# Step 3's decayed r and k are transposed by transfers, and the engine orders from word 50 on are new

## The chip, the cores and the metric

The kernel runs on one core of one Trainium2 chip. The metric is the device time of one execution in microseconds: 182.38 as the median of three runs of the kernel before (181.91 to 182.72). Five engines work side by side, each through its own queue in order: TensorE (PE, with its weight loads as PEld), VectorE (DVE), ScalarE (ACT), GpSimd (POOL) and SyncE (SP), which here issues all DMA transfers.

## What is computed

A linear attention with a decay per channel and a state (RWKV-6), and behind it a dense layer with squared relu:

```python
for t in range(S):                                   # B, H, S, D = 4, 8, 768, 48
    cur = einsum('bhd,bhe->bhde', u[None] * kt, vt)
    y[:, :, t] = einsum('bhd,bhde->bhe', rt, state + cur)
    state = wt[:, :, :, None] * state + einsum('bhd,bhe->bhde', kt, vt)
x = y as [3072, 384]
out = relu(x @ w_in) ** 2 @ w_out                    # w_in [384, 2048], w_out [2048, 384]
```

Inputs and output are float32; the matmuls run in bf16.

## The kernel before

The 3072 tokens are cut into 12 steps (0 to 11) of 256 tokens, three steps for each of the four sequences; a step has two chunks of 128, and each partition row holds two neighbouring tokens. For a step the attention goes this way: products of w (`ww_`), their logarithm (`lw_`), sums of it along the chunk by matmuls with triangles (`cum_`), the exponential (`exp_`, `ac_`), decayed r and k (`rd_.s.0` and `rd_.s.1`, lines 351 to 364), r and k transposed, their products for all pairs of tokens (`p_.s.0` and `p_.s.1`, line 420) times a mask (`pm_`), the states (`su_`, `ts_`, `sn_`), and y from the masked products and v (`y_`) and from r and the states (`yc_`), summed with a diagonal part (`q_`, `vq_`) in `ysb_`. For the dense layer y is transposed (`yt_` and its copy `xt_`, or one transfer, `dyt_`), multiplied with w_in in eight words of six matmuls (`m1_.s.0` to `m1_.s.7`, line 536), taken through relu (`rl_`) and square (`sq_.s.q`, each over two of the eight), multiplied with w_out in eight words of four matmuls (`m2_.s.c.q` for chunk c and quarter q, line 564), scaled (`os_`) and stored.

Decayed r and k can be transposed in two ways. `tr_` does it with eight matmuls against the identity into a PSUM bank (line 376), and `rkt_` copies the bank to SBUF (lines 391 and 393). `dtr_` issues one DMA that reads SBUF and writes SBUF:

```python
def dtr_(s, i):
    t = new_rkt(s, i)
    if i == 0:
        nc.sync.dma_start_transpose(out=t[:],
                                    in_=tiles["rdec", s][0][:].rearrange("t a j e d -> t (a j e d)"))
    else:
        nc.sync.dma_start_transpose(out=t[:].rearrange("p j a t -> p (j a) t"),
                                    in_=tiles["rdec", s][1][:].rearrange("t j h d -> t (j h d)"))
```

Before, steps 0 to 3 use `tr_` and `rkt_`, and steps 4 to 11 use `dtr_`.

Nothing is scheduled by a program at build time. The string ORDER lists words, and the loop at line 598 runs them one after the other; each appends its instructions to the queues of its engines. So the words' order is, engine by engine, the order of the instructions. A word reads `name.step.parts:bank=engine`: `rkt_.3.1=V` copies the transposed k (1; r is 0) of step 3 on VectorE (A is ScalarE, G is GpSimd). Banks `0` to `3` are single PSUM banks; `cum_`, `p_`, `su_` and `y_` use pairs of banks, `att0` and `att1` (`0` and `1` there), or the single banks in pairs (`b` is 0 and 1, `m` is 2 and 3). `warm_.n.i` are n matmuls on nothing that keep TensorE busy at the start. `ld.s.x` loads w, r, k or v of a step, or a part of w_in (`ld.n.i`) or w_out (`ld.n.o`), each of four; `cast.i.n` and `cast.o.n` make them bf16.

```python
for word in ORDER.split():
    word, _, engine = word.partition("=")
    word, _, banks = word.partition(":")
    name, *args = word.split(".")
    args = tuple(int(x) if x.isdigit() else x for x in args)
```

Of the kernel before, what the change touches and what calls it, by code (L numbers as in the profile page):

```python
# [20 lines left out]
ts_.0.0=A kw_.1=G pm_.0.0 pm_.0.1 vs_.0.0=A sn_.0.0 ld.1.i exp_.1 rw_.1=G vs_.0.1=A qs_.0=A rd_.1.1 ku_.1=G  # L21
warm_.3.2 yc_.0.1:1 ld.0.i ac_.1 ts_.0.1=V rd_.1.0 warm_.2.2 tr_.1.1:0 sn_.0.1 y_.0:1 rkt_.1.1=A vq_.0=V
tr_.1.0:1 ww_.2=G ld.2.i v_.1=A rkt_.1.0=V ysb_.0=V vs_.1.1=A warm_.4.2 p_.1.1:0 qp_.1=G su_.1:m ld.2.v
pm_.1.1 lw_.2 yt_.0:0 cum_.2:1 ld.3.i ts_.1.0=V rw_.2=G q_.1 exp_.2 kw_.2=G xt_.0=V vs_.1.0=A rd_.2.0 qs_.1=G
ac_.2 cast.i.1=A rd_.2.1 warm_.10.1 tr_.2.0:1 sn_.1.0 p_.1.0:0 ku_.2=G ts_.1.1=V yc_.1.1:1 tr_.2.1:0
cast.i.0=A pm_.1.0 ld.0.o m1_.0.3:2 ld.3.w rkt_.2.1=V m1_.0.2:3 vq_.1=G rkt_.2.0=V y_.1:1 rl_.0.3=A yc_.1.0:1
rl_.0.2=V p_.2.0:0 m1_.0.1:2 ld.1.o ysb_.1=V cast.i.2=G m1_.0.0:3 rl_.0.1=A pm_.2.0 yt_.1:0 ld.3.r rl_.0.0=A
m1_.0.5:2 v_.2=A xt_.1=V qp_.2=G sn_.1.1 m1_.0.4:3 rl_.0.5=A p_.2.1:1 su_.2:b sq_.0.0=A rl_.0.4=V ld.2.o
m1_.1.4:2 cast.i.3=G ts_.2.0=V pm_.2.1 m1_.1.5:3 rl_.1.4=A q_.2 sn_.2.0 m1_.1.3:2 rl_.1.5=A ld.3.o vs_.2.1=G
vs_.2.0=A yc_.2.0:0 yc_.2.1:0 rl_.1.3=V m1_.1.6:3 cast.o.0=G qs_.2=A m1_.1.0:2 ld.3.k rl_.1.6=V sq_.0.2=A  # L30
y_.2:0 rl_.1.0=V m1_.1.1:3 vq_.2=G m1_.1.7:2 rl_.1.1=V ld.3.v m2_.0.1.0:0 sq_.1.2=A rl_.1.7=V sq_.0.1=A
cast.o.1=G m1_.1.2:3 rl_.1.2=A ysb_.2=V m1_.0.7:2 ld.4.w ww_.3=G yt_.2:1 rl_.0.7=V m1_.0.6:3 xt_.2=V m2_.0.1.1
sq_.1.1=A rl_.0.6=V ld.5.w m1_.2.6:2 cast.o.2=G lw_.3 sq_.1.0=A rl_.2.6=A cum_.3:1 sq_.1.3=A rw_.3=G al_.3
ld.5.r m2_.0.0.0:1 m1_.2.7:3 m2_.0.0.1 cast.o.3=V exp_.3 sq_.0.3=A ld.4.k rd_.3.0 kw_.3=G m1_.2.1:2 rl_.2.7=A
ac_.3 m2_.0.1.2 m2_.0.0.2 rl_.2.1=V ku_.3=G m2_.0.0.3 rd_.3.1 ld.4.v m2_.0.1.3 vs_.3.0=A m1_.2.0:3 os_.0.1=V
qp_.3=G ld.5.v m1_.2.3:2 os_.0.0=V rl_.2.0=V tr_.3.1:0 rl_.2.3=A tr_.3.0:1 rkt_.3.1=V v_.3=A ld.4.r m1_.2.4:3
ww_.4=G rkt_.3.0=V m2_.1.0.0:0 rl_.2.4=A q_.3 ww_.5=G p_.3.1:0 vs_.3.1=A ld.6.k su_.3:1 pm_.3.1 p_.3.0:m
m2_.1.0.1 ts_.3.0=A lw_.4 sn_.3.0 ld.5.k pm_.3.0 m2_.1.0.2 qs_.3=A m2_.1.1.0:1 sq_.2.0=A vq_.3=G ts_.3.1=V
m2_.1.0.3 ld.6.w cum_.4:0 m2_.1.1.1 ku_.4=G ac_.4 al_.4 store.0.1 m1_.2.5:2 os_.1.0=A v_.5=A yc_.3.1:1 y_.3:1
lw_.5 kw_.4=G m1_.2.2:3 ld.6.r ysb_.3=V rl_.2.5=A m2_.1.1.2 exp_.4 sn_.3.1 rl_.2.2=V yt_.3:0 rw_.4=G cum_.5:1  # L40
xt_.3=V m2_.1.1.3 vs_.4.0=A ac_.5 sq_.2.1=A qp_.4=G al_.5 m1_.3.0:2 rd_.4.1 v_.4=A m1_.3.3:3 rd_.4.0 dtr_.4.1
m2_.2.0.0:0 rl_.3.0=A rw_.5=G rl_.3.3=A m2_.2.0.1 os_.1.1=V exp_.5 q_.4 dtr_.4.0 su_.4:0 sq_.2.2=A m1_.3.4:2
kw_.5=G rd_.5.0 ww_.6=G m2_.2.1.0:1 rl_.3.4=A ts_.4.0=V sq_.2.3=A m1_.3.5:3 vs_.4.1=A rd_.5.1 sn_.4.0
m2_.2.1.1 store.1.0 ts_.4.1=V rl_.3.5=V ku_.5=G m1_.3.6:2 store.1.1 m2_.2.1.2 qs_.4=A ld.7.w ld.6.v rw_.6=G
p_.4.1:1 rl_.3.6=A p_.4.0:0 pm_.4.1 pm_.4.0 m2_.2.1.3 lw_.6 vq_.4=G m1_.3.1:3 m1_.3.2:2 rl_.3.1=A su_.5:1
dtr_.5.1 dtr_.5.0 vs_.5.1=G sq_.3.0=A rl_.3.2=V yc_.4.0:0 yc_.4.1:0 sn_.4.1 y_.4:0 os_.2.1=V sq_.3.1=A
m1_.3.7:3 ysb_.4=V ld.7.v m2_.2.0.2 rl_.3.7=A ld.8.w kw_.6=G vs_.5.0=G yt_.4:1 ld.7.k sq_.3.3=A m2_.2.0.3
xt_.4=V cum_.6:0 al_.6 m1_.4.4:2 qp_.5=G os_.2.0=A ac_.6 m1_.4.7:3 ts_.5.0=V exp_.6 rl_.4.4=V m2_.3.0.0:1
rl_.4.7=A rd_.6.1 m1_.4.6:2 rd_.6.0 m2_.3.0.1 dtr_.6.1 m2_.3.1.0:0 ku_.6=G qp_.6=G sq_.3.2=A rl_.4.6=A q_.5
dtr_.6.0 p_.5.0:1 p_.5.1:0 vs_.6.0=A m1_.4.5:3 sn_.5.0 m2_.3.0.2 qs_.5=G rl_.4.5=A pm_.5.1 pm_.5.0 vq_.5=G  # L50
m1_.4.1:2 m1_.4.3:3 rl_.4.3=A store.2.1 ld.8.v m2_.3.0.3 rl_.4.1=V ld.8.k v_.6=A ww_.7=G y_.5:0 q_.6 os_.3.0=A
ld.7.r m1_.4.0:3 store.0.0 ld.9.k ww_.8=G yc_.5.0:0 qs_.6=A su_.6:1 yc_.5.1:0 ysb_.5=V vs_.6.1=A ts_.6.0=V
m1_.4.2:2 ld.8.r m2_.3.1.1 rl_.4.0=V yt_.5:1 xt_.5=V sn_.6.0 lw_.7 vq_.6=G rl_.4.2=A p_.6.0:0 m2_.3.1.2
sq_.4.3=A store.2.0 pm_.6.0 m1_.5.2:3 ku_.7=G m1_.5.6:2 ts_.6.1=V yc_.6.1:0 sq_.4.0=A rl_.5.2=A p_.6.1:1
rl_.5.6=A m2_.3.1.3 kw_.7=G pm_.6.1 sq_.4.2=A m1_.5.4:3 rw_.7=G m1_.5.3:2 os_.3.1=V rl_.5.4=A y_.6:0 sn_.6.1
rl_.5.3=A cum_.7:1 kw_.8=G ysb_.6=V al_.7 m2_.4.0.0:1 vs_.7.1=A m1_.5.7:3 m1_.5.5:2 v_.7=G dyt_.6 sq_.4.1=A
rl_.5.7=V qp_.7=G rl_.5.5=V m2_.4.1.0:0 exp_.7 ld.9.w ld.9.v m2_.4.0.1 ac_.7 rd_.7.0 sq_.5.1=A m2_.4.0.2
ku_.8=G rd_.7.1 sq_.5.3=A dtr_.7.0 m2_.4.0.3 m1_.5.0:3 lw_.8 m1_.5.1:2 rw_.8=G rl_.5.0=V su_.7:0 q_.7
rl_.5.1=A cum_.8:1 dtr_.7.1 m1_.6.3:3 qs_.7=A m1_.6.5:2 rl_.6.3=V ld.10.w qp_.8=G ac_.8 sq_.5.0=A m2_.4.1.1
os_.4.0=V ts_.7.0=V ld.11.w sn_.7.0 m1_.6.4:3 rl_.6.5=A al_.8 ww_.9=G m2_.4.1.2 ld.9.r rl_.6.4=V exp_.8  # L60
store.3.0 m2_.5.1.0:1 sq_.5.2=A rd_.8.1 ts_.7.1=V sn_.7.1 m1_.6.0:2 vs_.7.0=G vs_.9.1=A rd_.8.0 m2_.4.1.3
m2_.5.1.1 kw_.9=G rl_.6.0=A dtr_.8.0 p_.7.1:0 v_.8=A p_.7.0:1 vq_.7=G pm_.7.1 m1_.6.1:3 m2_.5.1.2 rl_.6.1=A
pm_.7.0 ku_.9=G m2_.5.1.3 sq_.6.0=A lw_.9 m1_.6.6:2 dtr_.8.1 store.3.1 q_.8 yc_.7.0:0 v_.9=A yc_.7.1:0
rl_.6.6=V rw_.9=G su_.8:1 y_.7:0 os_.5.1=A ts_.8.0=V m1_.6.2:3 ysb_.7=V os_.4.1=A cum_.9:1 m1_.6.7:2 al_.9
dyt_.7 m2_.5.0.0:1 rl_.6.2=V exp_.9 ww_.10=G rl_.6.7=V m2_.5.0.1 ac_.9 ld.10.r rd_.9.1 sq_.6.1=A sq_.6.2=A
sn_.8.0 qp_.9=G ld.10.k qs_.8=G store.4.1 m2_.5.0.2 ld.10.v rd_.9.0 m2_.5.0.3 m2_.6.1.0:0 vs_.8.1=G sq_.6.3=A
dtr_.9.0 vs_.8.0=A p_.8.0:m p_.8.1:0 pm_.8.0 su_.9:1 m2_.6.1.1 ts_.9.0=A pm_.8.1 m2_.6.1.2 lw_.10 m1_.7.4:2
rw_.10=G os_.5.0=V m1_.7.0:3 rl_.7.4=V sn_.9.0 vq_.8=G yc_.8.1:0 dtr_.9.1 yc_.8.0:0 rl_.7.0=V y_.8:0 m1_.7.1:2
q_.9 rl_.7.1=A ts_.9.1=V m2_.6.1.3 kw_.10=G ysb_.8=V m1_.7.7:3 sq_.7.0=A ww_.11=G cum_.10:1 dyt_.8 rl_.7.7=V
m1_.7.5:2 qs_.9=A al_.10 m2_.6.0.0:1 v_.10=G rl_.7.5=A m1_.7.2:3 exp_.10 ld.11.k vs_.9.0=G m2_.6.0.1 lw_.11  # L70
rd_.10.0 rd_.10.1 m1_.7.3:2 rl_.7.2=A vq_.9=G ac_.10 m2_.6.0.2 os_.6.1=A rl_.7.3=A vs_.10.0=A store.6.1
m1_.7.6:3 store.5.1 ku_.10=G m2_.6.0.3 vs_.10.1=A ld.11.r sn_.9.1 rl_.7.6=V m1_.8.5:2 dtr_.10.0 p_.9.1:0
rl_.8.5=A p_.9.0:1 qp_.10=G pm_.9.1 m1_.8.3:3 m2_.7.0.0:0 rl_.8.3=A pm_.9.0 m1_.8.4:2 sq_.7.1=A m1_.8.2:3
os_.6.0=A y_.9:0 sq_.7.3=A rl_.8.2=V yc_.9.1:0 rw_.11=G su_.10:1 m2_.7.1.0:1 sq_.7.2=A ts_.10.0=V ysb_.9=V
m2_.7.1.1 rl_.8.4=A ku_.11=G q_.10 m1_.8.7:3 dyt_.9 m1_.8.1:2 rl_.8.7=V cum_.11:0 dtr_.10.1 kw_.11=G sn_.10.0
rl_.8.1=A m2_.7.1.2 al_.11 m1_.8.0:3 exp_.11 ld.11.v qs_.10=G ts_.10.1=V sn_.10.1 vq_.10=G m1_.8.6:2 rl_.8.0=A
store.6.0 rd_.11.0 m2_.7.1.3 rl_.8.6=A rd_.11.1 m1_.9.4:3 sq_.8.0=A ac_.11 dtr_.11.0 m1_.9.1:2 qp_.11=G
rl_.9.4=V sq_.8.2=A m2_.7.0.1 os_.7.1=V p_.10.1:1 sq_.8.1=A p_.10.0:0 pm_.10.1 store.5.0 dtr_.11.1 store.7.1
m1_.9.0:3 v_.11=G pm_.10.0 vs_.11.1=G m2_.8.1.0:1 rl_.9.0=A rl_.9.1=A m2_.8.1.1 sq_.8.3=V m1_.9.5:3 m2_.7.0.2
m2_.7.0.3 os_.7.0=A yc_.10.0:1 yc_.10.1:1 rl_.9.5=V su_.11:0 y_.10:1 m1_.9.2:2 ysb_.10=V m1_.9.6:3 rl_.9.2=A  # L80
ts_.11.0=V dyt_.10 m2_.8.0.0:0 rl_.9.6=V sn_.11.0 m1_.9.3:2 q_.11 m2_.8.1.2 rl_.9.3=A yc_.11.0:1 vs_.11.0=A
p_.11.1:0 yc_.11.1:1 p_.11.0:m m2_.8.0.1 pm_.11.0 m2_.8.0.2 pm_.11.1 sq_.9.1=A m2_.8.0.3 m2_.8.1.3 qs_.11=A
sq_.9.0=A m1_.9.7:2 os_.8.1=A vq_.11=G y_.11:1 sq_.9.2=A rl_.9.7=V m1_.10.0:3 sq_.9.3=V m2_.9.0.0:1 rl_.10.0=A
m1_.10.5:2 os_.8.0=A store.8.0 store.8.1 m2_.9.0.1 m1_.10.4:3 rl_.10.5=A rl_.10.4=A sq_.10.2=V m2_.9.0.2
# [550 lines left out]
```

## Time and profile before

| | us |
|---|---|
| three timed runs, median | 182.38 |
| the profiled execution | 182.57 |
| its span, first to last instruction | 180.8 |
| TensorE busy | 171.2 |
| ScalarE, VectorE, GpSimd busy | 132.4, 129.7, 122.8 |

A page of the profile gives for each engine its busy time, share and instructions; the chain of waits follows back from the last instruction what released what. A group's row names the line, the engine, the operation, out<-in with the shapes, the count, and behind the bar the busy time, the mean length of one in ns, the idle time ahead of them and what ended it. Lines are those of the kernel before; the changed kernel has one line less in ORDER, so its lines are one lower.

### The profile page before, as it was taken

To read this page: it belongs to the slowest core of one execution; us is meant where nothing else is said; L and a number is where in the kernel's file an instruction comes from. 1 tells how busy PE (TensorE), PEld (TensorE's weight loads), DVE (VectorE), ACT (ScalarE), POOL (GpSimd) and SP (SyncE) were. 2 spreads that over 40 slices of the span, in tenths; PEclk is the share of its full clock that TensorE was granted. 3 is DMA by queue.
4 is the path that set the end of the run, shared out by engine and by line. 5 is a ranking of instruction groups with operands and counts; after the bars stand their busy time and mean duration, and the time that the engine had idled before them with its cause. 6 is when DMAs were issued, how large, how long until landed. Compare 5 with 4: busy or idle time off the path is not lost.

```text
span 180.8 us, 5682 instructions
## 1 busy us (share of the span) xinstructions
PE 171.2 (95%) x2382; PEld 123.2 (68%) x2385; DVE 129.7 (72%) x195; ACT 132.4 (73%) x235; POOL 122.8 (68%) x140
## 2 busy tenths in 40 slices
...
GB/s 147 270 261 232 221 369 350 340 332 302 228 271 217 280 228 215 208 218 255 270 137 237 197 287 101 303 141 143 190 106 244 92 47 0 92 151 22 0 87 130
DMA packets 78952, 35.81 MB, mean 198 GB/s; under 512 B 72144, under 2 KB 77392, under 8 KB 78928
## 3 DMA queue, kind: packets, MB, share of 16 engines
...
## 4 chain that ended last, share of the span: by engine, by line
PE 78%; SPq 10%; DMA 5%; ACT 4%; DVE 1%; issue 1%; ACTq 0%
PE bk L564 33%; PE m L536 33%; SPq L180 8%; DMA w_st<-in_moe_w_in_dram 5%; PE att L420 3%; PE att L483 3%; PE att L493 2%; PE att L446 1%; ACT gt L545 1%; PE bk L516 1%; PE att L328 1%; ACT wi_sb L202 1%; SPq L190 1%; SPq L207 1%; ACT gt L553 1%
## 5 line engine op out<-in xcount | busy, mean ns | idle before, releaser
L536 PE MATMUL m<-xT,wi_sb 128*128 128x256 bf16 x576 | 74.0, 273 | 0.8 <-ACT gt L545 0.7
L564 PE MATMUL bk<-wo_sb,gt 128*128 128x384 bf16 x384 | 72.0, 326 | 0.0
L536 PEld LDWEIGHTS <-wi_sb 128*128 128x128 bf16 x576 | 54.8, 98 | 12.5 <-issue 0.9
L564 PEld LDWEIGHTS <-gt 128*128 128x128 bf16 x384 | 36.9, 98 | 19.2
L545 ACT ACTIVATE gt<-m 128x512 f16<-128x512 f32 x56 | 32.9, 594 | 21.6 <-PE m L536 21.1
L553 ACT ACTIVATE gt<-gt 128x1024 bf16<-128x1024 f16 x42 | 43.3, 1051 | 1.4 <-DVE gt L547 1.1
L547 DVE TENSOR_SCALAR gt<-m 128x512 f16<-128x512 f32 x40 | 27.1, 687 | 9.6 <-PE m L536 9.3
L434 DVE TENSOR_TENSOR pmT<-att,mask 128x1024 bf16<-128x1024 f32 x20 | 23.9, 1218 | 3.9 <-PE att L420 3.9
L299 POOL TENSOR_TENSOR ku<-k_raw,u_bc 128x768 f32<-128x768 f32 x12 | 21.8, 1819 | 0.4 <-DMA u_bc<-in_u_dram 0.4
L304 POOL TENSOR_TENSOR ku<-ku,r_raw 128x768 f32<-128x768 f32 x11 | 20.6, 1877 | 0.2
L318 POOL TENSOR_TENSOR ku<-v_sh,qs 128x768 f32<-128x768 bf16 x11 | 16.2, 1477 | 4.9 <-ACT qs L279 4.8
L279 ACT CAST v_sh<-v_raw 64x384 bf16<-64x384 f32 x34 | 17.3, 508 | 0.4
L292 POOL TENSOR_TENSOR k_raw<-k_raw,w_raw 128x384 f32<-128x384 f32 x12 | 12.1, 1010 | 6.3 <-DMA k_raw<-in_k_dram 6.2
L461 POOL TENSOR_TENSOR S<-t_state,ac_buf 128x192 bf16<-128x192 f32 x20 | 10.2, 508 | 8.1 <-DVE t_state L456 5.7
L504 DVE TENSOR_TENSOR y_sb<-att,ku 128x768 bf16<-128x768 f32 x12 | 11.4, 954 | 5.5 <-PE att L483 1.7
L288 POOL TENSOR_TENSOR r_raw<-r_raw,w_raw 128x384 f32<-128x384 f32 x12 | 12.0, 997 | 3.6 <-DMA r_raw<-in_r_dram 3.6
L363 DVE TENSOR_TENSOR kdec_buf<-k_raw,att 128x768 bf16<-128x768 f32 x12 | 11.4, 950 | 3.5 <-ACT att L342 2.9
L360 DVE TENSOR_TENSOR rdec_buf<-r_raw,att 128x384 bf16<-128x384 f32 x24 | 12.2, 548 | 2.2 <-ACT ac_buf L348 1.1
L342 ACT ACTIVATE att<-att 128x768 f32<-128x768 f32 x12 | 9.6, 799 | 3.4 <-PE att L330 2.0
L571 ACT ACTIVATE o_sb<-bk 128x384 f32<-128x384 f32 x13 | 6.2, 484 | 7.3 <-PE bk L564 7.3
L309 DVE TENSOR_REDUCE q<-ku 128x16 f32<-128x768 f32 x12 | 11.3, 944 | 0.0
L581 PE MATMUL att<-warm 128*128 128x512 bf16 x27 | 8.9, 487 | 1.2 <-DVE half_ones L230 1.2
...
## 6 DMA issues: line engine op xcount, KB each, us to landing
...
w_st<-in_moe_w_in_dram SPq DMA_DIRECT2D x4, 768.0 KB, 9.8
w_st<-in_moe_w_out_dram SPq DMA_DIRECT2D x4, 768.0 KB, 9.0
...
```

What stands on the lines that cost most here:

```text
L180: nc.sync.dma_start(out=t[:, hs, at:at + 2, :].rearrange("p h j d -> p h (j d)"), in_=src[b, hs, i * T:(i + 1) * T, :].rearrange("h (p j) ...
L279: copy(out[j * Q:(j + 1) * Q, c], src[c * Q:(c + 1) * Q, :, j])
L299: tensor_mul("ku_", s, h)(tiles["ku", s][:, hs], raw["k", s][:, hs, 1:3, :], u_bc[:, hs, None, :].to_broadcast([C, n, 2, D]))
L304: tensor_mul("qp_", s, h)(ku, ku, raw["r", s][:, heads(h), 0:2, :])
L318: tensor_mul("vq_", s)(vq[:], tiles["vs", s][:], tiles["qs", s][:, :, :, None].to_broadcast([C, 2, H, D]))
L360: nc.vector.tensor_mul(rdec[0][:, ps, j, :, 0:D], x[:, :, j, :].rearrange("p (a e) d -> p a e d", e=2), dec.rearrange("p (a e) d -> p a e ...
L434: nc.vector.tensor_mul(pmT, ps_p[:].rearrange("p e (x t) -> p (e x) t", t=C), mk.to_broadcast([C, 8, C]))
L536: nc.tensor.matmul(ps1[:, j, :], wi_sb[:, n // 4, kk, n % 4 * 128:(n % 4 + 1) * 128], tiles["xT", s][:, :, kk, :], start=(kk == 0), stop=( ...
L545: nc.scalar.activation(rl, m1, AF.Relu, scale=RS)
L547: nc.vector.tensor_scalar(out=rl, in0=m1, scalar1=RS, scalar2=0.0, op0=ALU.mult, op1=ALU.max)
L553: nc.scalar.activation(gt, rl, AF.Square)
L564: nc.tensor.matmul(m2, gt[:, 4 * q + n, c * C:(c + 1) * C], wo_sb[:, 4 * q + n, :], start=(summed[s, c] == 1 and n == 0), stop=(summed[s, ...
```

## The change

All that differs is ORDER. Its first 50 words, up to `qs_.0`, are the same; behind them the words stand in a new order, with new engines and banks. Four words go and two come:

```diff
-tr_.3.1:0 tr_.3.0:1 rkt_.3.1=V rkt_.3.0=V
+dtr_.3.1 dtr_.3.0
```

Of all others there are as many as before. Some have another engine: relus (`rl_`) on ScalarE are 65 and were 56, squares there 37 and were 42; scalings (`os_`) there 17 and were 13; four words of `ku_` and `kw_` that GpSimd had go to VectorE, and three `qp_` too. `m1_` used banks 2 and 3 and `m2_` banks 0 and 1; now both use all four.

In three places the order shows what the prediction speaks of. The first is SP, the queue of all transfers, where step 3 ends and step 4 begins. Before (from v of step 3 on; then w of steps 4 and 5, r of 5, k of 4, and so on up to the first transposing transfer, of step 4):

```order
L180 DMA v_raw<-in_v_dram 128x8x96
L180 DMA w_raw<-in_w_dram 128x8x96 x2
L180 DMA r_raw<-in_r_dram 128x8x96
L180 DMA k_raw<-in_k_dram 128x8x96
L180 DMA v_raw<-in_v_dram 128x8x96 x2
L180 DMA r_raw<-in_r_dram 128x8x96
L180 DMA k_raw<-in_k_dram 128x8x96 x2
L180 DMA w_raw<-in_w_dram 128x8x96
L577 DMA out_dram<-o_sb 128x384
L180 DMA r_raw<-in_r_dram 128x8x96
L403 DMA_TRANSPOSE kT<-kdec_buf_108 128x8x128
```

And after, from v of step 3 too:

```order
L179 DMA v_raw<-in_v_dram 128x8x96
L195 DMA w_st<-in_moe_w_out_dram 128x4x384
L179 DMA r_raw<-in_r_dram 128x8x96
L195 DMA w_st<-in_moe_w_out_dram 128x4x384
L179 DMA w_raw<-in_w_dram 128x8x96
L402 DMA_TRANSPOSE kT<-kdec_buf_110 128x8x128
L399 DMA_TRANSPOSE rT<-rdec_buf_109 128x8x128
L179 DMA w_raw<-in_w_dram 128x8x96
L179 DMA k_raw<-in_k_dram 128x8x96
L179 DMA r_raw<-in_r_dram 128x8x96
```

The two transposing transfers of step 3 stand behind w of step 5 and ahead of w, k and r of step 4; before, all loads of step 4 were in the queue by then.

The second place is VectorE at the start, in step 1 and the first words of step 2 (`pmT` are mask products, `kdec` and `rdec` decayed k and r, `y_sb` is y, `gt` a relu's result). Before, from the first mask product of step 1:

```order
L434 TENSOR_TENSOR pmT_467<-att0_86,mask_100 128x1024
L456 TENSOR_TENSOR t_state_484<-S_369,m1_0_90 128x192
L309 TENSOR_REDUCE q_487<-ku_331 128x16
L521 COPY xT_491<-bk0_88 128x768
L360 TENSOR_TENSOR rdec_buf0_107<-r_raw_222,att1_87 128x4x2x48 x2
L363 TENSOR_TENSOR kdec_buf0_108<-k_raw_299,att1_87 128x16x48
L456 TENSOR_TENSOR t_state_543<-S_523,m1_1_91 128x192
L434 TENSOR_TENSOR pmT_467<-att0_86,mask_100 128x1024
L393 COPY kT_582<-bk0_88 128x1024
L391 COPY rT_592<-bk1_89 128x1024
L547 TENSOR_SCALAR gt_573<-m1_1_91 128x512
L504 TENSOR_TENSOR y_sb_652<-att1_87,ku_590 128x768
```

And after:

```order
L433 TENSOR_TENSOR pmT_441<-att1_87,mask_100 128x1024
L455 TENSOR_TENSOR t_state_482<-S_409,m1_0_90 128x192
L359 TENSOR_TENSOR rdec_buf0_107<-r_raw_222,att0_86 128x4x2x48 x2
L362 TENSOR_TENSOR kdec_buf0_108<-k_raw_299,att0_86 128x16x48
L455 TENSOR_TENSOR t_state_514<-S_489,m1_1_91 128x192
L433 TENSOR_TENSOR pmT_441<-att1_87,mask_100 128x1024
L392 COPY kT_584<-m1_1_91 128x1024
L503 TENSOR_TENSOR y_sb_611<-att0_86,ku_498 128x768
L433 TENSOR_TENSOR pmT_674<-att1_87,mask_100 128x1024
L520 COPY xT_677<-bk0_88 128x768
```

The reduction `q_.1`, the copy of the first y transposed and the copy of r of step 2 have left this stretch, and no relu stands in it any more.

The third place is ScalarE where the relus and squares of step 4 are (`gt_1558` before, `gt_1562` after; relus read a PSUM bank, squares read `gt`; `v_sh` and `v_bf` are casts of v). Before:

```order
L545 ACTIVATE gt_1558<-m1_1_91 128x512
L553 ACTIVATE gt_1251<-gt_1251 128x1024
L545 ACTIVATE gt_1558<-m1_0_90 128x512
L279 CAST v_sh_1644<-v_raw_1380 64x384 x2
L545 ACTIVATE gt_1558<-m1_1_91 128x512 x2
L274 CAST v_bf_1693<-v_raw_1380 128x8x2x48
L571 ACTIVATE o_sb_1715<-bk1_89 128x384
L279 COPY qs_1746<-q_1713 64x8 x4
L279 CAST v_sh_1644<-v_raw_1380 64x384 x2
L270 ACTIVATE lw_buf1_102<-ww_1695 128x8x48
L545 ACTIVATE gt_1558<-m1_0_90 128x512
L553 ACTIVATE gt_1558<-gt_1558 128x1024 x2
```

And after:

```order
L544 ACTIVATE gt_1562<-m1_1_91 128x512
L278 CAST v_sh_1675<-v_raw_1264 64x384 x4
L278 CAST v_sh_1712<-v_raw_1558 64x384 x2
L544 ACTIVATE gt_1562<-m1_0_90 128x512
L544 ACTIVATE gt_1562<-bk0_88 128x512
L273 CAST v_bf_1743<-v_raw_1558 128x8x2x48
L544 ACTIVATE gt_1562<-bk1_89 128x512
L544 ACTIVATE gt_1562<-m1_0_90 128x512
L552 ACTIVATE gt_1562<-gt_1562 128x1024
L453 COPY t_state_1807<-att1_87 128x192
L552 ACTIVATE gt_1562<-gt_1562 128x1024
```

Between the first relu of step 4 and its first square stood five casts of v, and now stand seven; the copies `qs_` and the logarithm that stood there have moved behind or ahead.

The words of TensorE that go with it, in ORDER, are few lines of the diff's new side: first step 3, then the dense layer of step 4.

```diff
+ld.5.w cast.o.2=A rw_.3=G sq_.0.2=V rd_.3.0 vs_.3.1=G sq_.1.2=V ts_.3.0=V ac_.3 ww_.5=V m2_.0.0.2 sn_.3.0
+sq_.2.3=A m2_.1.1.2 os_.0.0=A qp_.3=V ts_.3.1=V q_.3 os_.1.1=A dtr_.3.1 dtr_.3.0 m2_.0.1.2 p_.3.1:1 p_.3.0:0
...
+p_.6.1:0 qp_.6=V rl_.4.5=A sq_.4.3=A m1_.4.0:1 ww_.8=G xt_.5=V ts_.6.0=A sn_.6.0 m2_.4.0.3:2 m1_.5.2:3 ld.7.w
```

140 lines of the change are left out of this document (68 added, 72 removed).

## The prediction, made before the changed kernel ran

> **What bounds the kernel now.** I read the busy shares of the page first, then stretches by window, then the chain of waits, then the engines that feed TensorE. The first two views (a stretch's row has its mean length, then busy time and instructions of PE, PEld, DVE, ACT and POOL, the granted clock, the DMA share and GB/s):
>
> ```profile
> PE 171.2 (95%) x2382; PEld 123.2 (68%) x2385; DVE 129.7 (72%) x195; ACT 132.4 (73%) x235; POOL 122.8 (68%) x140
> ```
> ```profile
> 60.00:84.00 24.00, 24.00 (x409) 17.89 (x405) 20.47 (x31) 20.90 (x40) 22.93 (x27) 1.00 1.12 229
> 84.00:108.00 24.00, 24.00 (x367) 17.74 (x354) 19.89 (x30) 22.33 (x39) 21.37 (x21) 1.00 1.05 229
> 108.00:132.00 24.00, 23.92 (x384) 17.92 (x381) 19.42 (x30) 18.88 (x36) 20.43 (x25) 1.00 0.79 173
> ```
>
> TensorE is busy in all but 0.1 us from 60 to 132, at full granted clock, and no other engine is. "Busy" can hide waiting, because the ends of matmuls are modelled, so I check it by pace, in the chain of waits (start, length, what):
>
> ```profile
> 18.95 9.05 DMA w_st<-in_moe_w_in_dram
> 28.03 1.47 ACT wi_sb L202
> 29.50 0.51 ACT gt L545
> 30.05 1.47 PE m L536 x12
> 31.52 0.33 PE bk L516 x6
> ...
> 38.23 1.31 PE m L536 x12
> ...
> 50.57 0.89 PE bk L376 x16
> ...
> 170.26 7.16 PE bk L564 x44
> 177.50 0.49 ACT o_sb L571
> ```
>
> 44 matmuls of `m2_` in 7.16 us are 0.163 us each, so a word of four is 0.65 us. Twelve of `m1_` in 1.31 us are two words of 0.655. From 30.05 on the work is 94 words of `m1_` (61.6 us), 96 of `m2_` (62.4) and some 20 us of small matmuls of the attention, 144 to 145 us; the clock shows 30.05 to 177.4, 147.3. No more than 3 us of that is waiting or switching: **TensorE alone sets the time from 30 us to the end**. Ahead of 30 it is the second part of w_in: it lands at 28.0 and is cast by 29.5. The tail behind the last matmul (a scaling and a store) is the same in both versions.
>
> The Trainium skill, "Perfetto Trace Analysis", Identifying the Most-Contended Engine, speaks against this reading: matmul busy time is a bad measure, and the share of weight loads a better one. That share is 68% here, by which a third of TensorE would be free and matmuls taken away worth nothing; the sum below would be 0.9 higher, 183.1. The even 0.163 us a matmul decides against it here.
>
> **The change, part by part.** The sums stand against the profiled execution: 182.57 us, of which 180.8 are the span and 1.77 lie around it. The runs shown have the median 182.38, 0.2 less.
>
> *The transposes of step 3 leave TensorE.* Sixteen matmuls go, the row of 0.89 us at 50.57, in the stretch that TensorE sets: **−0.89**. The two copies out of PSUM go too, on VectorE (the second like the first):
>
> ```profile
> L391 DVE COPY rT<-bk 128x1024 bf16<-128x1024 bf16 x3 | 2.0, 680 | 0.0
> ...
> L391 ACT COPY rT<-bk 128x1024 bf16<-128x1024 bf16 x1 | 1.0, 1012 | 0.1
> ```
>
> Those 1.4 us of an engine that has 4 us of slack in each 24 count as 0.
>
> *The two transfers that come for them* stand in SP's one queue, now ahead of the loads of step 4. Rows of before, for issue and for landing:
>
> ```profile
> 33.99 3.42 SPq L196 DMA_DIRECT2D w_st<-in_moe_w_out_dram  x2
> ...
> 40.64 5.38 SPq L180 DMA_DIRECT2D w_raw<-in_w_dram  x2
> ...
> 62.73 1.33 SPq L403 DMA_TRANSPOSE kT<-kdec_buf  x1
> 64.18 1.27 SPq L400 DMA_TRANSPOSE rT<-rdec_buf  x1
> ```
> ```profile
> w_st<-in_moe_w_out_dram SPq DMA_DIRECT2D x4, 768.0 KB, 9.0
> ...
> kT<-kdec_buf SPq DMA_TRANSPOSE x8, 3.9
> rT<-rdec_buf SPq DMA_TRANSPOSE x8, 4.2
> ```
>
> A transpose takes 1.3 us to issue and 4 us from there to landing. Will it be there in time? The last load of w_out had 12 MB with it and ahead of it in before (12 loads of 0.39, u with 0.2, eight parts of weights of 0.79 and two more loads of 0.39); it was issued in the second half of the row at 33.99 and landed near 45. In the new order r of step 3 ends the same 12 MB (seven parts of weights, four loads of step 3): 45. GpSimd then has r·w behind three operations:
>
> ```profile
> L299 POOL TENSOR_TENSOR ku<-k_raw,u_bc 128x768 f32<-128x768 f32 x12 | 21.8, 1819 | 0.4 <-DMA u_bc<-in_u_dram 0.4
> ...
> L288 POOL TENSOR_TENSOR r_raw<-r_raw,w_raw 128x384 f32<-128x384 f32 x12 | 12.0, 997 | 3.6 <-DMA r_raw<-in_r_dram 3.6
> ...
> L279 POOL CAST v_sh<-v_raw 64x384 bf16<-64x384 f32 x14 | 7.5, 537 | 0.6
> ...
> L274 POOL CAST v_bf<-v_raw 128x768 bf16<-128x768 f32 x3 | 2.5, 818 | 0.0
> ```
>
> 0.82 + 1.82 + 2 × 0.54 + 1.00 = 4.7 us, from about 42.5 (v lands 2.5 us before r): 47.2. VectorE has four operations of 0.69 ahead of the decayed r, behind an `m1_` that ends at 45.3: 48.1, and with its own 1.1 it is done at 49.2. It lands at 49.2 + 4.2 = 53.4. TensorE comes to the `p_` words of step 3 after 20 `m1_`, 14 `m2_` and 2.3 us of small words: 30.0 + 13.1 + 9.1 + 2.3 = 54.5. That leaves 1.1 us, so I cost the transfers at **0**; what hides them are those 14 words of `m2_`. The ends are 0, since nothing here shortens TensorE's work, and +3 (the queue rival below).
>
> *The start.* From the 50th word on the order is new. VectorE now has eight operations between the first `p_` of step 1 and the transpose of that step's y, and ScalarE comes later to r of step 1, because it first waits for v:
>
> ```profile
> 19.09 0.83 ACT L274 CAST v_bf<-v_raw 128x768 bf16<-128x768 f32 x1 [0.94 <-DMA v_raw<-in_v_dram]
> 19.95 1.03 ACT L279 CAST v_sh<-v_raw 64x384 bf16<-64x384 f32 x2
> 21.00 0.52 ACT L270 ACTIVATE lw_buf<-ww 128x384 bf16<-128x384 f32 x1
> ```
> ```profile
> L434 DVE TENSOR_TENSOR pmT<-att,mask 128x1024 bf16<-128x1024 f32 x20 | 23.9, 1218 | 3.9 <-PE att L420 3.9
> ...
> L360 DVE TENSOR_TENSOR rdec_buf<-r_raw,att 128x384 bf16<-128x384 f32 x24 | 12.2, 548 | 2.2 <-ACT ac_buf L348 1.1 <-ACT att L342 1.0
> ...
> L504 DVE TENSOR_TENSOR y_sb<-att,ku 128x768 bf16<-128x768 f32 x12 | 11.4, 954 | 5.5 <-PE att L483 1.7 <-POOL ku L299 1.3 <-PE att L493 1.3
> L363 DVE TENSOR_TENSOR kdec_buf<-k_raw,att 128x768 bf16<-128x768 f32 x12 | 11.4, 950 | 3.5 <-ACT att L342 2.9 <-POOL S L461 0.4 <-issue 0.3
> ...
> L456 DVE TENSOR_TENSOR t_state<-S,att 128x192 f32<-128x192 bf16 x12 | 4.2, 347 | 1.0 <-POOL S L461 0.8 <-PE att L446 0.3
> ```
>
> ScalarE: 19.1 + 0.83 + 1.03 + 0.2 + 0.52 + 1.01 (the copy of r) = 22.7, and 0.4 for the matmuls of `p_`: VectorE begins at 23.1. Its row is 1.22 + 0.35 + 1.10 + 0.95 + 0.35 + 1.22 + 0.68 + 0.95 = 6.8, so y of step 1 stands at 29.9 by full durations, and at 29.2 if each begins 0.1 before the one ahead ends, as the rows at 19.09 and 21.00 show between neighbours elsewhere; the transpose adds 0.33. The first `m1_` on the second part of w_in can't start before its cast ends, 29.5. So that stream starts between 29.5 and 30.3; I take 30.0, which is before's 30.05. It has one transpose of y less to do, the row of 0.33 at 31.52, which now stands ahead of it: **−0.33**, with ends −0.9 and 0. Of the products that change from GpSimd to VectorE, u·k has no row there: between the 0.95 of y's sum and the 1.22 of the mask, and I take 0.95; VectorE idles behind the one of step 1, so either gives 0.
>
> *Waits that the new order brings.* I looked for words of TensorE whose input is made shortly before, and three stand out.
>
> 1. Squares on ScalarE. From the last `m1_` of a square to the first `m2_` that reads it there are 3.0 us of TensorE's work or less at four places (steps 4, 5, 7, 8) and 3.1 at a fifth; in before 3.8 at least, but for 3.25 at the very end. At step 4 ScalarE has from the first relu on 8 relus, 3 casts of v by rows of two halves, one cast, 4 squares, a copy and 2 logarithms:
>
> ```profile
> L553 ACT ACTIVATE gt<-gt 128x1024 bf16<-128x1024 f16 x42 | 43.3, 1051 | 1.4 <-DVE gt L547 1.1
> ...
> L545 ACT ACTIVATE gt<-m 128x512 f16<-128x512 f32 x56 | 32.9, 594 | 21.6 <-PE m L536 21.1
> ```
> ```profile
> 86.22 1.99 ACT L553 ACTIVATE gt<-gt 128x1024 bf16<-128x1024 f16 x2
> ```
>
> 8 × 0.594 + 3 × 1.03 + 0.83 + 4 × 1.05 + 0.3 + 2 × 0.52 = 14.2 us, where TensorE has 9 `m1_`, 4 `m2_` and 3.4 us of small words, 11.9. By full durations that is 2.3 late. But two squares took 1.99, not 2.10; with 0.1 off for each of the 19, it is 12.3. I take **+0.3**, between 0 and +2.3.
>
> 2. `p_.6.0` goes to the PSUM pair of `p_.6.1` and must wait for its mask product, which has a cast of v ahead of it on VectorE: **+0.2** (0 to 1).
> 3. `p_.10.1` goes to a bank that `m2_.8.1` holds until its scaling (0.49), 0.2 us of TensorE's work earlier: **+0.4** (0 to 0.6).
>
> The sum: 182.57 − 0.89 − 0.33 + 0.9 = 182.25, **182.2**. A measurement of this kernel tells about 0.5% (0.9 us) from no change, so this is "the same", leaning to faster.
>
> **Rivals.** *The order fits everywhere* (faster). The three waits are covered: 182.57 − 1.22 = 181.35, and 180.8 if the stream starts at 29.5 too. For it speaks that before, as dense, waits 3 us at most; against it, the five places at 3.1 or less. Chance 0.28.
>
> *ScalarE falls behind at the squares* (slower). Relu and square take 0.59 + 1.05 = 1.64 us, so with 3.0 us of distance the point from which it decides is some 1.35 us of lateness in ScalarE's queue, and its idle time is small: 1.7 of 24 us in the stretch 84 to 108. Behind that point TensorE waits for what is over. If one stretch runs late by the full 2.3, the time is 182.2 − 0.3 + 2.3 = 184.2; two give 186.5. Chance 0.26.
>
> *The transposes hold up the queue* (slower). If the decayed r of step 3 comes 2 us later, `p_` waits 0.9; and the load of w of step 4, issued in the row at 40.64 before and now not ahead of 49.2 + 1.3 = 50.5, delays that step's sums by up to 2 more: 183.1 to 185. For it speaks that this queue was full (two issues took 5.38). Chance 0.12.
>
> The Trainium skill, "VectorE: DVE Perf Modes", The three transpose paths, speaks against the change: TensorE where the result may go to PSUM, at 390 ns a block of 128×128, against 1309 ns by transfer. By that, as an estimate, eight blocks need 10.5 us and `p_` of step 3 waits some 5 us more: 187. The rows here (16 blocks in 0.89 us on TensorE, 4 us for eight by transfer) leave it 0.01, inside the rival above.
>
> That the change doesn't take the work away is excluded: the order has 16 matmuls less on TensorE and two transfers more.
>
> **How the numbers follow.** Forecast 0.34 (181.5 to 183.4, likeliest 182.2); all covered 0.28; late squares 0.26; late queue 0.12. Faster by over 0.5% (under 181.5) is the second case, 0.28; slower by over 0.5% the last two, 0.38; within it, 0.34. The range for 8 in 10 leaves out the best end of the covered case and the far end of the late squares: 180.8 to 185.8. The forecast's own is 181.5 to 183.4.
>
> **What would show it.** Right: no transposes of step 3 at TensorE, the stream starting from 29.5 to 30.3, TensorE at 24 of 24 in each stretch, and behind 30 us a chain of waits of TensorE alone. Late squares: rows of ScalarE's squares in that chain, and its wait for `m1_` well under 21 us. Late queue: TensorE waiting for a transfer near 54. Wrong altogether: a stream that starts after 31, or waits that I didn't name of over 3 us.

## The result: slower by 1%, and the profile after

| | before | after |
|---|---|---|
| median, us (19 executions each) | 182.44 | 184.28 |
| lowest to highest | 181.59 to 183.58 | 183.16 to 185.74 |
| ratio | | 1.0104, 95% interval 1.0082 to 1.0126 |
| the profiled execution (its span) | 182.57 (180.8) | 183.19 (181.4) |

The forecast was 182.2, "the same", with 181.5 to 183.4 as its own range. The time rose by 1.8 us. The ratios here and below leave out executions over 1.5% above the fastest of the same kernel (one of six in `dtr3_alone` and in `dtr3_first`), and they are not quotients of the medians. The profiled execution of the changed kernel is one of the shortest of its 19, so its trace shows the least of what went wrong. The busy shares and the granted clock, from its page:

```profile
PE 170.5 (94%) x2367; PEld 122.9 (68%) x2369; DVE 133.2 (73%) x200; ACT 133.8 (74%) x238; POOL 114.7 (63%) x133
...
PEclk9996999999999999999999999999999999999999
```

TensorE is busy 0.7 us less: the sixteen matmuls are gone. The three stretches that were full in before, now (columns as there):

```profile
60.00:84.00 24.00, 23.94 (x376) 17.89 (x375) 20.96 (x33) 20.26 (x42) 19.07 (x18) 1.00 1.13 225
84.00:108.00 24.00, 23.84 (x370) 17.18 (x369) 19.35 (x29) 21.10 (x36) 17.29 (x26) 1.00 1.14 237
108.00:132.00 24.00, 22.58 (x325) 17.37 (x323) 19.10 (x29) 20.04 (x39) 19.23 (x17) 1.00 1.02 216
```

One of them lacks 1.4 us, and TensorE's waits name it (engine, line, for what: us in total, times, longest):

```profile
PE att L492 <- DVE pmT L433: 1.6, 1, 1.6
PE att L325 <- ACT lw_buf L269: 1.5, 2, 1.3
PE att L419 <- DMA rT<-rdec_buf: 1.4, 1, 1.4
```

The first two lie ahead of 22 us, before the stream of `m1_` and `m2_` starts. The third is `p_` waiting for a transposing transfer. The chain of waits, with the places that the prediction spoke of:

```profile
29.51 0.42 PE bk L515 x6
29.94 0.65 PE m L535 x6
...
65.82 5.20 DMA kT<-kdec_buf
...
71.07 0.43 PE att L419 x16
...
85.46 1.07 ACT gt L552
...
86.57 0.82 PE m L563 x4
...
123.98 5.73 DMA rT<-rdec_buf
129.85 0.65 PE att L419 x32
```

The stream starts at 29.8, about as worked out (its first matmul at 29.77; the chain counts it from the end of the one ahead, 29.94). Step 3 is not in the chain: its transfers landed at 50.7 and 52.9, and `p_` came at 55.1. The squares of step 4 are in it (0.27 us over the usual pace of the `m1_` ahead). Two transposing transfers are in it that the prediction did not time: k of step 4 (0.2 us) and r of **step 9**, whose 5.73 us end 1.6 us after the last `m1_` ahead of it would have let `p_` go.

The table shows, for the later of each step's two transposing transfers, how long before the step's first `p_` it landed in the traces. Steps 4 to 11 go by transfer in both kernels.

| step | 3 | 4 | 5 | 6 | 7 | 8 | 9 | 10 | 11 |
|---|---|---|---|---|---|---|---|---|---|
| before | | 0.8 | 3.4 | 3.2 | 1.7 | 3.6 | 5.1 | 1.6 | 5.3 |
| after | 2.3 | 0.0 | 2.0 | 0.8 | 0.3 | 1.3 | 0.1 | 2.2 | 2.7 |

A margin of 0.0 or 0.1 means that `p_` was waiting. In before nothing is under 0.84; the new order has less than that at four steps (4, 6, 7 and 9; step 6 has 0.75).

### The profile page after: what moved, and what is told of

Read it like the earlier page. It is cut to its first block, busy times and chain, and to the rows that moved or that the text cites. A ratio compares the mean times of both kernels' runs of the same rounds, so it can differ in the third digit from the quotient of the medians.

```text
span 181.4 us, 5659 instructions
## 1 busy us (share of the span) xinstructions
PE 170.5 (94%) x2367; PEld 122.9 (68%) x2369; DVE 133.2 (73%) x200; ACT 133.8 (74%) x238; POOL 114.7 (63%) x133
## 4 chain that ended last, share of the span: by engine, by line
PE 73%; DMA 10%; ACT 6%; SPq 5%; DVE 2%; issue 1%; DVEq 0%; ACTq 0%
PE m L563 19%; PE bk L535 15%; PE bk L563 15%; PE m L535 12%; SPq L179 5%; DMA v_raw<-in_v_dram 4%; DMA rT<-rdec_buf 3%; DMA kT<-kdec_buf 3%; PE att L482 2%; PE att L419 2%; ACT v_sh L278 2%; PE att L492 2%; PE att L445 1%; ACT gt L544 1%; PE bk L580 1%
## 5 line engine op out<-in xcount | busy, mean ns | idle before, releaser
L535 PE MATMUL bk<-xT,wi_sb 128*128 128x256 bf16 x324 | 42.5, 273 | 0.1
L563 PE MATMUL m<-wo_sb,gt 128*128 128x384 bf16 x224 | 42.0, 326 | 0.1
L552 ACT ACTIVATE gt<-gt 128x1024 bf16<-128x1024 f16 x37 | 38.1, 1053 | 1.5 <-DVE gt L546 1.1
L535 PE MATMUL m<-xT,wi_sb 128*128 128x256 bf16 x252 | 33.6, 273 | 0.0
L563 PE MATMUL bk<-wo_sb,gt 128*128 128x384 bf16 x160 | 30.0, 326 | 0.0
L544 ACT ACTIVATE gt<-bk 128x512 f16<-128x512 f32 x37 | 21.8, 595 | 6.5 <-PE bk L535 6.2
L544 ACT ACTIVATE gt<-m 128x512 f16<-128x512 f32 x28 | 16.5, 595 | 7.5 <-PE m L535 7.2
L546 DVE TENSOR_SCALAR gt<-bk 128x512 f16<-128x512 f32 x17 | 11.6, 686 | 7.9 <-PE bk L535 7.8
L303 POOL TENSOR_TENSOR ku<-ku,r_raw 128x768 f32<-128x768 f32 x8 | 14.5, 1816 | 1.0 <-DVE ku L298 0.9
L570 ACT ACTIVATE o_sb<-m 128x384 f32<-128x384 f32 x10 | 4.9, 490 | 12.6 <-PE m L563 12.5
```

What stands on the lines that cost most here:

```text
L303: tensor_mul("qp_", s, h)(ku, ku, raw["r", s][:, heads(h), 0:2, :])
L535: nc.tensor.matmul(ps1[:, j, :], wi_sb[:, n // 4, kk, n % 4 * 128:(n % 4 + 1) * 128], tiles["xT", s][:, :, kk, :], start=(kk == 0), stop=( ...
L544: nc.scalar.activation(rl, m1, AF.Relu, scale=RS)
L546: nc.vector.tensor_scalar(out=rl, in0=m1, scalar1=RS, scalar2=0.0, op0=ALU.mult, op1=ALU.max)
L552: nc.scalar.activation(gt, rl, AF.Square)
L563: nc.tensor.matmul(m2, gt[:, 4 * q + n, c * C:(c + 1) * C], wo_sb[:, 4 * q + n, :], start=(summed[s, c] == 1 and n == 0), stop=(summed[s, ...
```

## Experiments

Theory 1: the time is lost at transposing transfers of later steps, that of step 9 above all, since the new order puts them closer to their use. Theory 2: the new order is tight in many places, and no single one matters. Theory 3: the transfers of step 3 themselves, in SP's queue, push back what is behind them. Each kernel was timed beside the kernel before on the same chip.

### A second look at the changed kernel

> The changed kernel with no edit, for a second look at its waits, because the profiled execution (183.19 us) lies 1.1 below the median of its runs (184.28). Theory 1, the transposing transfer of decayed r of step 9 comes late: p_ of step 9 waits again, 1.6 us as in the first profile at 183.2, and up to 2.7 where the execution takes 184.3. Theory 2, the new order is tight in many places: that wait stays at 1.6 or less, and what is added lies in other waits of 0.1 to 0.5 each. Time against the kernel before: 1.008 to 1.013 by both.

Measured: 184.67 (183.17 to 185.84), ratio 1.0125 (1.008 to 1.017). This profiled execution took 185.84, the longest. From its chain of waits, and the stretch 24 to 30:

```profile
108.56 5.05 DMA kT<-kdec_buf
...
113.65 0.43 PE att L419 x16
...
126.34 5.97 DMA rT<-rdec_buf
...
132.44 0.65 PE att L419 x32
```
```profile
24.00:30.00 6.00, 6.00 (x95) 3.56 (x93) 4.19 (x8) 4.39 (x5) 5.29 (x7) 0.75 1.13 333
```

Against the first profile it has two things more. The stream starts 1.85 later: the granted clock is 0.75 in 24 to 30, while in the first profile the low stretch lay at 15.0 to 18.5, where TensorE has time to spare. And `p_` of step 8 also waits for its transfer (1.0), which landed 5.05 after its issue began instead of 3.2. Step 9 waits 1.4 again. Theory 1 had that wait grow with the time, and it did not; theory 2 had small waits of 0.1 to 0.5 added, and what came was a late start and one more late transfer.

### The transfer of step 9 one place ahead

```diff
-m1_.7.4:1 ld.11.r sn_.9.0
+m1_.7.4:1 sn_.9.0
...
-rd_.10.0 dtr_.9.0 ts_.9.1=V
+rd_.10.0 dtr_.9.0 ld.11.r ts_.9.1=V
```

> The changed kernel with one word moved: in SP's queue the transposing transfer of decayed r of step 9 stands ahead of the load of r of step 11 instead of behind it; all else as in the change. Theory 1, that transfer is what the time is lost to: it lands at least one issue (0.6 us) and one load's transfer (about 1.2) earlier, the wait of 1.6 at p_ of step 9 goes or falls under 0.3, and the time falls by 1.3 to 2.5 from 184.3, to 181.8 to 183.0, 0.997 to 1.003 of the kernel before. Theory 2, many tight places: the next one takes the time up, and it stays above 183.7, 1.007 or more.

Measured: **182.48** (182.11 to 183.96), ratio 1.0030 (1.0003 to 1.0058). SP's queue in the changed kernel and in this one (start, length, line, what):

```profile
121.50 1.76 SPq L402 DMA_TRANSPOSE kT<-kdec_buf  x1
123.35 0.53 SPq L179 DMA_DIRECT2D r_raw<-in_r_dram  x1
123.98 1.86 SPq L399 DMA_TRANSPOSE rT<-rdec_buf  x1
```
```profile
121.81 2.13 SPq L402 DMA_TRANSPOSE kT<-kdec_buf  x1
124.04 1.25 SPq L399 DMA_TRANSPOSE rT<-rdec_buf  x1
125.39 0.54 SPq L179 DMA_DIRECT2D r_raw<-in_r_dram  x1
```

And TensorE there, first the changed kernel, then this one:

```profile
127.61 0.82 PE L535 MATMUL bk<-xT,wi_sb 128*128 128x256 bf16 x6
129.85 0.65 PE L419 MATMUL att<-rT,kT 64*64 64x128 bf16 x32 [1.42 <-DMA rT<-rdec_buf]
```
```profile
127.88 0.82 PE L535 MATMUL bk<-xT,wi_sb 128*128 128x256 bf16 x6
128.86 0.69 PE L419 MATMUL att<-rT,kT 64*64 64x128 bf16 x32 [0.16 <-DVE rdec_buf L359]
```

The transfer lands at 127.36 instead of 129.72, and what `p_` waits for now is the bank, which the decayed r of step 10 reads last. One transfer moved by one place takes the ratio from 1.0104 and 1.0125 to 1.0030: of the 1.9 to 2.3 us that the change had cost, 1.4 to 1.7 come back, the size of the wait. Theory 1 holds for most of the loss; theory 2 is left with the rest, some 0.5 us.

The load ahead costs more than its own issue. Behind it r of step 9 took 5.65 to 5.97 us from issue to landing in all four traces of kernels with that order, and 3.3 to 5.2 in the six where it stands ahead of the load.

### The transfers of step 3, in the new order

In `tr3_back` the first part of the change is undone alone; in `r9_tr3` that is done on `r9_ahead`.

```diff
-dtr_.3.1 dtr_.3.0
+tr_.3.1:4 tr_.3.0:5 ... rkt_.3.1=A ... rkt_.3.0=V
...
-        return quad[int(i)][:].bitcast(BF16)
+        return (quad + [att[0][:, e, :] for e in range(2)])[int(i)][:].bitcast(BF16)
```

> The changed kernel with the first part of the change undone alone: r and k of step 3 are transposed by 16 matmuls and two copies again, in the two banks of att0, which are free there, and the two transfers leave SP's queue; the rest of the new order stays. If the transfers of step 3 are hidden as the prediction had it and the loss comes later, TensorE has 0.89 us more to do and the time rises by 0.9, to 185.2 (1.014 to 1.018). If those transfers hold up SP's queue and so the later steps (theory 3), the time stays or falls: 184.3 or less.

> Both edits on the changed kernel at once: r of step 9 goes ahead of the load (as in r9_ahead) and r and k of step 3 are transposed by 16 matmuls and two copies again (as in tr3_back). With the wait of step 9 out of the way, the price of the transfers of step 3 alone is seen against r9_ahead (182.5). If they are hidden, taking them back costs TensorE 0.89 us: 183.4 (1.007 of the kernel before). If they delay the later transfers in the queue by more than TensorE gains (theory 3), the time is 182.5 or less.

Measured: `tr3_back` 183.85 (183.68 to 184.53), ratio 1.0098 (1.0073 to 1.0123), not 185.2; `r9_tr3` 183.06 (182.31 to 184.73), ratio 1.0062 (1.0036 to 1.0088), which is 0.6 above `r9_ahead`. While step 9 waits, giving 0.89 us of work back to TensorE costs nothing in the ratio. Two readings fit. In the trace of `tr3_back` the wait at step 9 is 0.8 instead of 1.4 to 1.6, so that **a saving ahead of a wait can go into the wait**. And that of step 4 is gone: without the transfers of step 3 the margins at steps 4 to 7 are 1.7, 4.2, 2.6 and 1.4, where the changed kernel has 0.0, 2.0, 0.8 and 0.3. That is theory 3, which had forecast 184.3 or less here; as far as these runs go, it holds for the margins. These runs don't part the two. With the wait of step 9 gone, giving the work back costs 0.6, so the 16 matmuls are then a saving, and theory 3 does not explain the loss. Its size is less sure: the intervals of `r9_tr3` and `r9_ahead` overlap, and in the trace of `r9_tr3` a wait of 0.6 at the transposed y of step 7 stands in the place of 0.4 and 0.3 at `p_` of steps 4 and 9.

### The transfers of step 3, in the old order

```diff
-rd_.3.0 kw_.3=G
+rd_.3.0 dtr_.3.0 kw_.3=G
-rd_.3.1 ld.4.v
+rd_.3.1 dtr_.3.1 ld.4.v
-tr_.3.1:0 rl_.2.3=A tr_.3.0:1 rkt_.3.1=V
+rl_.2.3=A
-rkt_.3.0=V m2_.1.0.0:0 rl_.2.4=A q_.3 ww_.5=G p_.3.1:0
+m2_.1.0.0:0 rl_.2.4=A q_.3 ww_.5=G m2_.1.0.1 m2_.1.0.2 p_.3.1:0
```

> The kernel before with the first part of the change alone: two transposing transfers for step 3 in SP's queue, r behind the load of r of step 5 and k behind the load of k of step 4, in place of 16 matmuls and two copies; the products p_ of step 3 stand two m2_ words later, and no other word is moved. If the transfers are hidden, TensorE does 0.89 us less and the time is 182.4 - 0.9 = 181.5 (0.995). If the queue pays for them (theory 3), p_ of step 3 or the first sums of step 4 wait for transfers by 1 us or more and the time is 182.4 or above.

Measured: 185.99 (183.95 to 186.71), ratio 1.0182 (1.0137 to 1.0228): in the old order, at these places, the transfers cost time. The chain of its profiled execution (186.71, the longest), and its stretch 54 to 66:

```profile
51.88 4.61 DMA kT<-kdec_buf
...
56.53 0.43 PE att L420 x16
```
```profile
54.00:66.00 12.00, 9.66 (x154) 6.33 (x153) 6.24 (x10) 7.62 (x18) 7.54 (x7) 0.86 1.23 242
```

`p_` of step 3 waits 2.5 us for k. Its source was ready at 49.1, but r's transfer held SP's queue to 51.8, and k's then took 4.6 us, behind loads that were still landing 1.4 us apart. And the wait is paid twice: behind it the granted clock is 0.86 over 12 us, 12 × 0.14 = 1.7 us of TensorE's time, and the four words behind the wait lose about that (0.30 + 0.61 + 0.63 + 0.20).

`dtr3_first` puts the two transfers ahead of the loads of r of step 5 and k of step 4. With them v of step 4 moves back too, behind r of step 4:

```diff
-rw_.3=G al_.3 ld.5.r m2_.0.0.0:1
+rw_.3=G al_.3 m2_.0.0.0:1
...
-ld.4.k rd_.3.0 dtr_.3.0 kw_.3=G
+rd_.3.0 dtr_.3.0 kw_.3=G
-rd_.3.1 dtr_.3.1 ld.4.v
+rd_.3.1 dtr_.3.1 ld.4.k
-ld.4.r m1_.2.4:3
+ld.4.r ld.4.v ld.5.r m1_.2.4:3
```

> dtr3_alone with SP's queue in another order: the two transposing transfers of step 3 stand ahead of the loads of r of step 5 and k of step 4, which move behind them, so that two loads less are in front. If the wait at p_ of step 3 (2.51 us) comes from those loads, the transfers land some 2.8 us earlier, the wait goes, and so does the low clock behind it: 181.5 to 182.2 (0.995 to 0.999 of the kernel before). If a full queue takes them no sooner, or the loads put back come late for step 4, it stays at 184 or above.

Measured: 185.10 (183.88 to 186.66), ratio 1.0163 (1.0118 to 1.0208). The wait of step 3 is gone (k lands at 51.5, `p_` at 52.9), and step 4 has it instead:

```profile
52.45 7.28 DMA v_raw<-in_v_dram
...
66.36 3.13 DMA rT<-rdec_buf
...
69.63 0.65 PE att L420 x32
```

v of step 4, which the edit itself had moved back, and then r's transposing transfer of step 4 are late, 1.9 us at `p_`. In this queue a transfer put ahead is paid for by those behind it. The new order has fewer loads ahead of step 3's transfers, and by the trace of `tr3_back` it pays with the margins of steps 4 to 7.

### Does a wait of TensorE bring the clock down?

`dtr3_warm` is `dtr3_alone` with 11 matmuls on nothing in the wait:

```diff
-m2_.1.0.2 p_.3.1:0
+m2_.1.0.2 warm_.11.4 p_.3.1:0
```

> dtr3_alone with 11 matmuls on nothing (512 columns, about 0.23 us each) ahead of p_ of step 3, where TensorE waited 2.51 us for the transfers; all else the same. In dtr3_alone the words right behind that wait ran slow (0.30, 0.61, 0.63 and 0.20 over their usual times, with a granted clock of 0.86 in 54 to 66). If the wait itself brought the clock down, TensorE kept busy keeps it at 1.00, the words behind run at their usual times, and the time falls by some 1.7 from 186.0, to 184.3. If the clock falls by chance, the time stays at 185.5 or above.

Measured: 184.65 (183.99 to 185.29), ratio 1.0141 (1.0117 to 1.0164), with a mean granted clock of 1.00 in all six executions (0.991 in four of the six of `dtr3_alone`: 185.9 to 186.7; the two at 1.00 took 183.95 and 184.87). The stretch:

```profile
54.00:66.00 12.00, 12.00 (x175) 7.81 (x173) 7.65 (x13) 8.77 (x20) 7.74 (x7) 1.00 1.13 247
```

`p_` starts 2.5 us behind the last word of the dense layer as before (its transfer lands no sooner), and the words behind it run at their usual times. So the wait can bring the clock down, and 0.7 (by the ratios, whose intervals overlap) to 1.3 us (by the medians) of the loss was that. Within `dtr3_alone` the four executions at the low clock are 1.0 to 2.8 us longer than the two at 1.00. The Trainium skill, "TensorE: Matmul & The Clock Gate", Part 1: The HAM clock gate, says that the gate halves the clock after an idle window of some 3.4 us; here an idle time of 2.5 us was enough in four executions of six, and behind it the granted clock is at 0.50 for some 3.4 us (57.2 to 60.6 in the trace of `dtr3_alone`).

The same for the start of the new order, where TensorE waits 1.6 and 1.9 us (13 matmuls on nothing more, `warm_.5.2` ahead of `yc_.0.1` and `warm_.12.2` for `warm_.4.2`), on `r9_ahead` and on the changed kernel:

> r9_ahead with 13 more matmuls on nothing in the two longest idle stretches of TensorE at the start: 5 ahead of yc_ of step 0 (idle 1.56 us ahead of 14.96) and 8 more ahead of the sums of step 2 (idle 1.94 ahead of 21.50). If those idle stretches are what brings the granted clock down for some 3.4 us in most executions of the new order (8 of 12 of r9_ahead at 0.991 or less), and those where it falls into 24 to 30 are the longer ones (183.2 to 184.0), the clock stays at 1.00 in nearly all, the long ones vanish, and the median falls from 182.5 to 182.1 (1.000). If the clock falls by chance, nothing changes: 182.5 (1.003), with the same share of low clocks.

> The changed kernel with the same 13 matmuls on nothing at the start and nothing else. It parts the loss of the change between the clock and the late transfer. If the clock at the start is the part above the profiled execution (183.2), the executions of 184.5 to 185.8 vanish and the median falls from 184.5 to about 183.2 to 183.5 (1.006 to 1.008), the late transfer of step 9 staying with its 1.4 to 1.6 us. If the late transfers alone make the long executions, the median stays at 184.3 or more (1.012).

Measured: `r9_warm` 182.79 (182.23 to 184.22), ratio 1.0037 (1.0012 to 1.0061); `after_warm` 184.06 (183.13 to 184.93), ratio 1.0114 (1.0086 to 1.0143). The clock did as expected: 0.997 or more in all 18 executions, where it was 0.991 or less in 24 of 25 of the changed kernel and in 8 of 12 of `r9_ahead`. The time did not follow clearly: `r9_warm` is no faster than `r9_ahead`, and the intervals of `after_warm` and of the changed kernel overlap. The low clock at the start, which the new order has nearly always, costs nothing that shows where it falls at 15 to 18 us: the stream starts at 29.77 in the first profile, and at 29.87 in that of `r9_ahead`, whose clock is 1.00. Where it falls at 24 to 27, as in the execution of 185.84, the stream starts 1.85 later. None of the six executions of `after_warm` was over 185, and 5 of 25 of the changed kernel were; six are too few to tell. But executions of 184.2 and 184.9 came at a clock of 1.00 as well. What lengthens those is seen in the chain of `r9_warm`:

```profile
107.08 4.94 DMA kT<-kdec_buf
...
112.06 0.43 PE att L419 x16
```

The transfer of k of step 8 took 4.94 us here (3.35 in `r9_ahead`, at the same place in the queue), and `p_` waited 0.9.

### Taking out the other waits

`waits_out` is `r9_ahead` with six moves at the waits that its trace still has, `fit_warm` is `r9_warm` with them and one of them mended.

```diff
-yt_.2:1 sq_.1.0=V xt_.2=V
+yt_.2:1 xt_.2=V sq_.1.0=V
-ld.6.w store.0.1 su_.4:0 ... dtr_.4.1 ld.6.k
+ld.6.w su_.4:0 ... dtr_.4.1 store.0.1 ld.6.k
-y_.5 vs_.6.1=A rl_.4.7=A ... ww_.8=G xt_.5=V
+y_.5 rl_.4.7=A ... ww_.8=G vs_.6.1=G xt_.5=V
-ld.9.k p_.7.0:1 yc_.7.0:0 yc_.7.1 dtr_.8.0 m1_.6.7:2 ... store.4.1 pm_.7.0 dtr_.8.1
+p_.7.0:1 m1_.6.7:2 yc_.7.0:0 yc_.7.1 dtr_.8.0 dtr_.8.1 ld.9.k ... store.4.1 pm_.7.0
-p_.9.0:0 vs_.9.1=V p_.9.1:1 m1_.8.7:0
+m1_.8.7:0 p_.9.0:0 vs_.9.1=V p_.9.1:1
```

> r9_ahead and the other waits of TensorE in its trace taken out by moving words: the copy xt_ of step 2 ahead of a square on VectorE (wait 0.36); a store behind the two transposing transfers of step 4 (0.38); the cast of v of step 6, second chunk, from ScalarE to GpSimd (squares of step 4, 0.27); p_ of step 7 and yc_ of step 7 one m1_ apart (0.24); the transfers of step 8 together, ahead of a load and a store; one m1_ ahead of p_ of step 9 (0.33). If these waits are what holds r9_ahead above the sum of TensorE's work, the time falls by up to 1.6, to 180.9 to 181.5 (0.994 to 0.997 of the kernel before). If what is taken out only comes back a few words later, it stays at 182.2 or more.

Measured: 183.68 (182.95 to 185.13), ratio 1.0095 (1.0060 to 1.0131): worse than `r9_ahead`. Two moves brought larger waits than they took. (The profiled execution, the longest, also starts its stream 1.8 late at a low clock in 24 to 27.) VectorE:

```profile
70.34 0.95 DVE L362 TENSOR_TENSOR kdec_buf<-k_raw,att 128x768 bf16<-128x768 f32 x1
72.92 0.56 DVE L572 TENSOR_SCALAR o_sb<-m 128x384 f32<-128x384 f32 x1 [1.63 <-PE att L419]
```

The scaling `os_` stands still for 1.63 us. The row names a matmul that it does not read; the store that I had put behind the transfers landed at 72.83 and held the buffer that `os_` writes. Behind it stood a relu, and a `p_` of step 4 waited 1.5 for that relu's bank. With a cast of v on GpSimd the squares of step 4 no longer wait (0.3), and `p_` of step 6 waits 0.4 to 0.5 for its mask product instead; so it does in `fit_warm`. That is the second of the three waits of the prediction, which the squares had covered.

> r9_warm with the moves of waits_out, one of them mended: there the store of step 0 behind the transfers of step 4 kept its buffer, and a scaling on VectorE waited 1.63 us for it and held a relu that p_ of step 4 needs; now the store stays where it was, and the load of w of step 6 goes behind the transfers instead. If that store was what spoilt waits_out, the waits of 0.24 to 0.38 go and the time is 181.0 to 181.6 (0.994 to 0.997 of the kernel before). If every move brings a new wait of its size, it stays at 182.1 or above, as r9_warm.

Measured: 184.92 (184.07 to 185.64), ratio 1.0169 (1.0136 to 1.0203): worse again. Now the load that I had put behind the transfers held up GpSimd, in the chain of waits:

```profile
66.62 5.02 DMA w_raw<-in_w_dram
...
71.70 1.00 POOL ww L265
72.71 1.43 POOL ku L317
74.14 1.79 POOL ku L298
...
76.00 1.82 POOL ku L303
...
79.69 0.56 DVE xT L520
...
80.30 0.83 PE m L535 x6
```

GpSimd stood still for that load at a product with w, three products ran late behind it, then the sum `q_` on VectorE and the copy `xt_` behind that, and TensorE waited 1.9.

The last kernel keeps `r9_ahead` and the moves that had brought no wait (the first, the fourth and the fifth of the diff):

> r9_ahead with only those moves that took a wait out and brought none of their own in the traces so far: the copy xt_ of step 2 ahead of a square on VectorE (0.36); one m1_ between p_ and yc_ of step 7 (0.24); the two transfers of step 8 together, ahead of a load and a store (0.9 to 1.0 in those executions where they land late, about a third); one m1_ ahead of p_ of step 9 (0.33). The store ahead of step 4's transfers and the cast of v of step 6 stay as in the change. If the waits left in r9_ahead are separate and can be taken out one by one, the time falls by 0.9 to 1.2 from 182.5, to 181.3 to 181.6 (0.995 to 0.998 of the kernel before), and its spread narrows. If the order is so dense that each comes back elsewhere, it stays at 182.3 or above (1.001 or more).

Measured: **182.04** (181.61 to 183.86), ratio 1.0008 (0.9983 to 1.0033): the same as before. Its stretches:

```profile
60.00:84.00 24.00, 23.79 (x376) 17.83 (x374) 20.81 (x33) 20.10 (x42) 18.93 (x18) 1.00 1.14 222
...
108.00:132.00 24.00, 23.93 (x363) 18.46 (x363) 20.34 (x31) 20.60 (x40) 19.52 (x16) 1.00 1.03 225
```

The moves gave 0.4 of the 0.9 to 1.2 hoped for, and the intervals of `fit` and `r9_ahead` overlap. What is left in its trace is `p_` of step 4 (0.4, its transfer) and the squares of step 4 (0.3). No kernel here beats the one before.

## Why the prediction was wrong, step by step

- *TensorE sets the time from 30 us on.* Right, but for waits that the new order adds. The sixteen matmuls were worth some 0.6 of their 0.89 once step 9 no longer waited (`r9_tr3` against `r9_ahead`, intervals overlapping). By the Trainium skill's rule ("Perfetto Trace Analysis", Identifying the Most-Contended Engine) they would have been worth nothing; these runs lean against it.
- *The transfers of step 3 cost nothing at step 3.* Right, with more in hand than worked out: they landed at 52.9 (53.4 was predicted), and `p_` came at 55.1 (54.5). The estimate of 10.5 us for eight blocks by the Trainium skill ("VectorE: DVE Perf Modes", The three transpose paths) did not come true: r's transfers took 3.1 to 5.7 from issue to landing.
- *The start.* Right: 29.8 for 30.0, and the y of step 1 set it, done at 29.4 (29.2 to 29.9 was predicted). The other bound, the cast of the second part of w_in, was done at 28.5 and not at 29.5. The overlap of 0.1 between neighbours is not in the two rows of ScalarE that were named for it (19.92 to 19.95, 20.98 to 21.00); VectorE has some 0.1 of it there.
- *Squares of step 4, +0.3.* Right: 0.27. *`p_.6.0`, +0.2, and `p_.10.1`, +0.4.* Both were covered: TensorE was not idle ahead of either.
- *"I looked for words of TensorE whose input is made shortly before, and three stand out."* **This step failed.** I had timed the transfers that the change adds, and not the sixteen that it moves. Those of steps 4 to 11 stand in the new order too, closer to their use, and at step 9 with a load in between. The waits that this brings were put at nothing. From its first matmul to the start of the last scaling the stream took 147.45 before (30.05 to 177.50) and 148.33 in the first profile after (29.77 to 178.10), with 1.24 less to do (0.89 of step 3, 0.35 of the transpose of y that now stands ahead of it): 2.1 us more of waits. Some 1.5 of them are at step 9, 0.3 at the copy of step 2, 0.3 at the squares, and 0.1 to 0.2 each at k of step 4 and at step 7; before had 0.4 of waits that are gone. With the start's 0.28, 182.57 − 0.89 − 0.35 − 0.28 + 2.1 = 183.15; the execution took 183.19. The 1.1 us from there to the median are not in this profile; the traces of longer executions show more late landings (step 8) and, in one, the low clock at the start.
- It could have been seen. From the word `rd_.9.0` to `p_.9` TensorE has eight words of 0.65 and one of 0.37, 5.6 us. SP has k's transfer and a load to issue ahead of r's, 1.3 + 0.6, and then the 4.2 of r's own, 6.1: 0.5 late by medians alone.
- And medians are too small a number for a margin. The answer on rT in the first profile after:

```profile
DMA to landing us min/median/max: 3.1/4.6/5.7
```

  With 5.7 in place of 4.2 the sum above is 2.0 late; some 1.5 to 1.6 was measured.
- *Late queue* (183.1 to 185) is the rival whose range holds the time, and transposing transfers did come late. But its price was worked out from the decayed r of step 3 and the load of w of step 4. Step 3 had 2.3 us in hand, and the waits came at step 9, and at 8 and 4. That the price fits is luck.
